# A fused attention, expert and feed-forward kernel: a feed-forward weight piece in five bit operations instead of six, with two pieces fetched ahead instead of four

## The chip, the cores and the metric

The kernel runs on one core of one Trainium2 chip. The metric is the device time of one execution in microseconds. The engines are named as in the profile: PE is TensorE (PEld its weight loads), DVE is VectorE, ACT is ScalarE, POOL is GpSimd and SP is SyncE, whose queue issues most transfers.

## The reference

```python
x = attention(q, k, v, f)                 # causal softmax with a decay, 4 x 8 heads, 576 x 64
x = x.transpose(0, 2, 1, 3).reshape(2304, 512)
logits = x @ w_gate + modality_bias[modality_id]
e_idx = argmax(logits, axis=1)            # one of 8 experts for each token
gate_w = softmax(logits)[e_idx]
for e in range(8):
    h = maximum(x[e_idx == e] @ w1[e], 0)             # 512 -> 1024
    out[e_idx == e] = gate_w * (h @ w2[e])            # 1024 -> 512
h = out @ w_in                                        # 512 -> 2048
g = maximum(h, 0) + alpha * minimum(h, 0)
return g @ w_out                                      # 2048 -> 512
```

The two feed-forward weights `w_in` and `w_out` arrive as 64-bit floats: they are drawn as 32-bit numbers and divided by a 64-bit square root. The kernel reads each number as two 32-bit words, `lo` and `hi`, and rebuilds a 32-bit float from them: the sign and the top exponent bit of `hi`, the next 27 bits of `hi` shifted left by 3, and the top 3 bits of `lo`.

## The kernel before, in words

Products are computed in pairs of 16-bit numbers, a high part and the rest (`split`), so that each matrix product is three matmul passes. Attention and routing fill the first part of the program. Tokens are then gathered by expert into slots of 128 rows. The changed code lies in the loop at L1529, which runs once for each of the last 14 slots, `s` from 6 to 19. All five engines run in the order in which the program is written (`manual_schedule`), so an instruction that waits holds up everything behind it on its engine or queue.

One pass of the loop does the following. POOL gathers the tokens of slot `s + 4`. PE computes the first expert product of slot `s + 1` in two halves (`hidden`, L1197), and ACT (L1204) and DVE (L1205) turn each half into the 16-bit pair `hs`. SP issues a transposing transfer for the tokens of slot `s + 3` (`xturn`, L1180) and two for the pair of slot `s + 1` (`hturn`, L1218, `ht<-hs`). PE then computes the second product of slot `s` (`outer`, L1232), which reads the `ht` of that slot; ACT (L1244) and DVE (L1245) write its result `yr`, and POOL scatters it (L1249). `hs` and `ht` have two buffers each. After slot 14 SP also fetches the first rows for the feed-forward stage (`fetch_rows` of `x2a`, L1424), which needs the scatters so far.

Between these steps the loop prepares weights. `work` (L1502) is a list of 34 pieces: 26 feed-forward pieces, and after every third of them one of 8 pieces of a third expert's weights. So pieces 1, 5, 9, 13, 17, 21, 25 and 29 are expert pieces. Each piece has three steps: a fetch on SP of 512 KB into one of four buffers (`ffn_fetch` L1441, `part_fetch` L190 and L193); a second step (`ffn_bits` on DVE, or `part_hi`, two copies on ACT, L1492 and L1493); and a third (`ffn_split`: two ACT copies, L1475 and L1476, and a POOL subtraction, L1477; or `part_lo`: one POOL subtraction, L1498). `convert` with counter `k_` runs the second step of piece `k_`, the third step of piece `k_ - 1`, and one fetch. The counter `due` places one or two calls of `convert` ahead of `outer` and one or two behind it, mostly three in a pass. The calls are placed, by piece: slot 6: 0, 1 and 2; slot 7: 3, 4 and 5; slot 8: 6 and 7, 8; slot 9: 9 and 10; slot 10: 11, 12 and 13; slot 11: 14 and 15, 16; slot 12: 17 and 18, 19; slot 13: 20 and 21; slot 14: 22, 23 and 24; slot 15: 25 and 26, 27; slot 16: 28 and 29; slot 17: 30, 31 and 32; slot 18: 33 (the word "and" stands for `outer`).

A buffer of the four comes free when its feed-forward piece has been through `ffn_bits`, or its expert piece through `part_lo`, one call of `convert` later.

The feed-forward stage behind the loop prepares six more pieces with the same `ffn_bits` and `ffn_split` (`late_step`, L1707), between its own products (`ffn_in`, L1669, L1674 to L1682).

Of the kernel before, what the change touches and what calls it, by code (L numbers as in the profile page):

```python
# [17 lines left out]
ALU = mybir.AluOpType  # L18
# [70 lines left out]
LEAST = struct.unpack("f", struct.pack("I", 897 << 20))[0]  # L89
# [3 lines left out]
def kernel(  # L93
# [17 lines left out]
    nc = tc.nc  # L111
    B, H, S, D = q.shape
    N, DM = out.shape
    E, _, F = w1.shape
# [1151 lines left out]
    def wsel(s):  # L1266
        if s < NX:
            c = s // NA
            return (lambda m, kk, cs_: w1c[:, c, m, kk, cs_]), (lambda m, kk: w2c[:, c, m, kk, :])
        if s == NS - 1:  # L1270
            return (lambda m, kk, cs_: w1x[:, m, kk, cs_]), (lambda m, kk: w2x[:, m, kk, :])
        if s not in cvs:
            cvs[s] = nc.tensor.value_load(cri[0:1, s - NX:s - NX + 1], min_val=0, max_val=1)
        cv = cvs[s]
        return (
            (lambda m, kk, cs_: w1c[:, bass.ds(cv, 1), m, kk, cs_]), (lambda m, kk: w2c[:, bass.ds(cv, 1), m, kk, :])
        )
# [168 lines left out]
    def ffn_bits(g, raw):  # L1446
        lo, hi = raw[:, :, 0], raw[:, :, 1]
        ta = cvs2[0].tile([P, 512], U32, tag="ta", name="ta")
        tb = cvs2[0].tile([P, 512], U32, tag="tb", name="tb")
        tk = ta.bitcast(F32)  # L1450

        nc.vector.tensor_scalar(out=ta, in0=hi, scalar1=0x7FFFFFFF, scalar2=None, op0=ALU.bitwise_and)  # L1452
        nc.vector.tensor_scalar(  # L1453
            out=tb, in0=hi, scalar1=0x80000000, scalar2=0x40000000, op0=ALU.bitwise_and, op1=ALU.bitwise_or
        )
        nc.vector.tensor_scalar(out=tk, in0=tk, scalar1=LEAST, scalar2=None, op0=ALU.max)  # L1456
        nc.vector.scalar_tensor_tensor(  # L1457
            out=tb, in0=lo, scalar=29, in1=tb, op0=ALU.logical_shift_right, op1=ALU.bitwise_or
        )
        nc.vector.tensor_scalar(  # L1460
            out=ta, in0=ta, scalar1=3, scalar2=0x7FFFFFFF, op0=ALU.logical_shift_left, op1=ALU.bitwise_and
        )
        nc.vector.tensor_tensor(out=ta, in0=ta, in1=tb, op=ALU.bitwise_xor)  # L1463
        return tk

    def ffn_split(g, tk):
# [36 lines left out]
    for g in range(KH + 16 - LATE):  # L1503
        work.append((lambda g=g: ffn_fetch(g), lambda t, g=g: ffn_bits(g, t), lambda t, g=g: ffn_split(g, t)))
        if g % PS == 0 and g // PS < KD + KF // 2:
            y = g // PS
            work.append((lambda y=y: part_fetch(ex2, y), lambda t, y=y: part_hi(y, t), lambda t, y=y: part_lo(y, t)))
# [3 lines left out]
    def fetch():  # L1511
        if at_[0] < len(work):
            got[at_[0]] = work[at_[0]][0]()
            at_[0] += 1

    def convert():
        k_ = at_[1]
        if k_ < len(work):
            got[k_] = work[k_][1](got[k_])
        if 0 <= k_ - 1 < len(work):  # L1520
            work[k_ - 1][2](got.pop(k_ - 1))
        fetch()
        at_[1] += 1

    for _ in range(4):
        fetch()
    per = len(work) / (NS - NX - 0.5)
    due = 0.0
    for s in range(NX - 1, NS):  # L1529
        if s + 4 < NS:  # L1530
            gather(s + 4, *colof(s + 4))
        if s + 1 < NS:
            m1, _ = wsel(s + 1)
            hidden(s + 1, 0, m1)
            hidden(s + 1, 1, m1)
            if s + 3 < NS:
                xturn(s + 3)
            hturn(s + 1)
        due += per / 2
        while at_[1] < min(due, len(work)):  # L1540
            convert()
        outer(s, wsel(s)[1])
        if s == NS - 6:

            fetch_rows(x2a, 0, G0)
            fetch_tokens(0, G0)
        due += per / 2
        while at_[1] < min(due, len(work)):
            convert()
    while at_[1] <= len(work):  # L1550
        convert()
# [6 lines left out]
    with tc.If(more > 0):  # L1558
# [3 lines left out]
        for e in range(E):  # L1562
# [7 lines left out]
            out=inb, in0=jr, in1=sx[:, :, 0:1].rearrange("p e o -> p o e").to_broadcast([P, 32, E]), op=ALU.is_ge  # L1570
        )
        nc.vector.tensor_tensor(
            out=inb2, in0=jr, in1=sx[:, :, 1:2].rearrange("p e o -> p o e").to_broadcast([P, 32, E]), op=ALU.is_ge
# [11 lines left out]
            out=ro, in0=ro, in1=sx[:, :, 0:1].rearrange("p e o -> p o e"), op=ALU.subtract  # L1585
# [19 lines left out]
        for c in (1, 2):  # L1605
            nc.vector.scalar_tensor_tensor(
                out=off[:, 0, :], in0=sel[:, c, :], scalar=noff[:, c - 1:c], in1=off[:, 0, :], op0=ALU.mult, op1=ALU.add
# [4 lines left out]
            out=inb2, in0=inb2, scalar=float(P), in1=off.to_broadcast([P, 32, E]), op0=ALU.mult, op1=ALU.add  # L1612
# [94 lines left out]
    def late_step():  # L1707
        if lbits:
            g, tk = lbits.pop(0)
            ffn_split(g, tk)  # L1710
        if lraw:
            g, raw = lraw.pop(0)
            lbits.append((g, ffn_bits(g, raw)))
        if late:
            g = late.pop(0)
            lraw.append((g, ffn_fetch(g)))
# [50 lines left out]
```

## Time and profile before

| | us |
|---|---|
| runs of the kernel | 931.6, 944.95, 931.2 (median 931.6) |
| the profiled execution | 936.06 |
| its span in the profile | 934.3 |

| engine | busy us | share of the span |
|---|---|---|
| PE | 805.8 | 86% |
| DVE | 530.4 | 57% |
| ACT | 347.6 | 37% |
| POOL | 343.3 | 37% |

The shares are means over stages with different limits: the loop with the changed code lies between about 376 and 541 us of the span. A row of the timeline gives start, duration, engine, line, operation, the tiles written and read, the count, and in brackets how long the engine had been idle and what released it. A row of waits gives the total, the number of times and the longest. The names of releasers are inferred; where a named engine had long been done, it was another.

### The profile page before, as it was taken

How to read it: one execution, taken by the hardware profiler on the slowest of the kernel's cores; microseconds unless marked ns; L12 is line 12 of the kernel's file. 1: busy time of each engine (PE TensorE's matmuls, PEld its weight loads, DVE VectorE, ACT ScalarE, POOL GpSimd, SP SyncE). 2: the span in 40 equal slices, each digit the busy share in tenths (PEclk: the TensorE clock that was granted, in tenths of full speed). 3: DMA queues.
4: the chain of work that ended last, by engine and by line, in shares of the span. 5: the costliest groups of instructions: out<-in, count | busy, mean ns of one | idle time of the engine just before them, and what ended most of it. 6: DMA issues, size and time to landing. Idle time of an engine off the chain costs nothing. (4 is left out here: it accounts for less than half of the span.)

```text
span 934.3 us, 15725 instructions
## 1 busy us (share of the span) xinstructions
PE 805.8 (86%) x5565; PEld 448.9 (48%) x5565; DVE 530.4 (57%) x1236; ACT 347.6 (37%) x670; POOL 343.3 (37%) x387
## 2 busy tenths in 40 slices
PE   4887958596997874989887999899999999999995
PEld 3776746474775432434332474344444444444442
DVE  6987869694875554588997869633035105402400
ACT  4885747564755323445453323211012102201200
POOL 4544344352435225545553444423124114302400
PEclk9998888897999987989998999999999999999998
DMA  7889999999761896999989344002002000000000
GB/s 149 171 148 187 161 127 209 179 151 159 126 113 41 153 130 166 274 220 222 248 221 233 92 123 114 12 12 46 24 22 46 12 23 12 1 23 22 1 23 22
DMA packets 226632, 103.17 MB, mean 110 GB/s; under 512 B 192843, under 2 KB 213944, under 8 KB 226554
## 3 DMA queue, kind: packets, MB, share of 16 engines
q1 hardware_dynamic: 221018, 87.29, 50.2%
q0 software_dynamic: 5536, 14.86, 5.2%
q8 instruction: 46, 0.75, 0.4%
q14 instruction: 32, 0.26, 0.1%
HBM read 49.06 MB, written 15.59 MB: 69 GB/s over the span
## 5 line engine op out<-in xcount | busy, mean ns | idle before, releaser
L1674 DVE TENSOR_SCALAR t<-a,al 128x512 f32<-128x512 f32 (+1 forms) x80 | 55.6, 696 | 208.4 <-PE a L1669 208.4
L1669 PE MATMUL a<-x,wi 128*128 128x512 f16 x768 | 166.7, 379 | 0.1
L1669 PEld LDWEIGHTS <-wi 128*128 128x128 f16 x960 | 94.7, 99 | 98.6 <-issue 5.3
L1232 PE MATMUL y<-wcc,ht 128*128 (+1 forms) x456 | 113.0, 405 | 33.3 <-DMA ht<-hs 33.2
L1691 PEld LDWEIGHTS <-g 128*128 128x128 f16 x864 | 84.9, 98 | 106.9 <-issue 6.1
L1682 POOL TENSOR_TENSOR g<-t,g 128x512 f16<-128x512 f32 (+1 forms) x80 | 85.4, 1068 | 116.0 <-ACT g L1681 113.0
L1691 PE MATMUL o<-wo,g 128*128 128x512 f16 x540 | 120.7, 382 | 0.0
L1197 PE MATMUL h<-wcc,xgt 128*128 (+1 forms) x456 | 105.9, 387 | 16.2 <-POOL wcc L1399 13.2
L1681 ACT ACTIVATE g<-t 128x512 f16<-128x512 f32 (+1 forms) x80 | 46.9, 587 | 156.4 <-DVE t L1677 151.7
L1232 PEld LDWEIGHTS <-ht 128*128 128x128 f16 x480 | 48.8, 103 | 98.8 <-DMA ht<-hs 39.6
L651 ACT ACTIVATE t<-e,nm 128x512 f32<-128x512 f32 (+2 forms) x144 | 81.3, 602 | 21.2 <-DVE e L628 13.8
L663 PE MATMUL pt<-identf,t 128*128 128x128 f32 x384 | 65.6, 296 | 24.5 <-ACT t L651 16.1
L1197 PEld LDWEIGHTS <-xgt 128*128 128x128 f16 x480 | 47.2, 99 | 73.3 <-issue 17.2
L679 DVE SCALAR_TENSOR_TENSOR p<-pt,p 128x512 f16<-128x512 f32 x96 | 65.4, 682 | 25.6 <-ACT p L672 25.0
L1691 PE MATMUL o<-wob,g 128*128 128x512 f16 x324 | 73.6, 380 | 3.4 <-ACT wob L1475 1.8
L1698 POOL DMA_INDIRECT out_dram<-ob,tka x18 | 17.6, 976 | 155.1 <-ACT ob L1696 155.1
L1696 ACT ACTIVATE ob<-o 128x512 f32<-128x512 f32 x18 | 10.7, 597 | 162.5 <-PE o L1691 162.5
L628 DVE TENSOR_SCALAR_CACHE_REDUCE e<-s 128x512 f32<-128x512 f32 (+3 forms) x128 | 58.0, 480 | 3.9 <-PE s L581 3.9
L672 ACT ACTIVATE p<-pt 128x512 f16<-128x512 f32 x96 | 56.1, 585 | 3.6 <-PE pt L663 3.3
L663 PEld LDWEIGHTS pt<-identf,t 128*128 128x128 f32 x384 | 43.3, 149 | 28.3 <-ACT t L651 19.6
L1677 DVE SCALAR_TENSOR_TENSOR t<-a,t 128x512 f32<-128x512 f32 (+1 forms) x80 | 51.0, 638 | 2.8
L580 PE MATMUL s<-yw,wcc 128*128 128x256 f16 (+1 forms) x192 | 48.1, 275 | 4.9 <-DMA yw<-wcc 4.9
(317 smaller groups left out, 1219.3 us busy)
## 6 DMA issues: line engine op xcount, KB each, us to landing
raw<-in_moe_w_in_dram SPq DMA_DIRECT2D x16, 512.0 KB, 6.7
raw<-in_moe_w_out_dram SPq DMA_DIRECT2D x16, 512.0 KB
yw<-wcc SPq DMA_DIRECT2D x14, 320.0 KB, 5.2
kn<-in_k_dram SPq DMA_DIRECT2D x16, 256.0 KB, 4.1
qn<-in_q_dram SPq DMA_DIRECT2D x32, 128.0 KB, 4.2
vn<-in_v_dram SPq DMA_DIRECT2D x16, 256.0 KB, 3.1
xs<-nat SPq DMA_DIRECT2D x16, 256.0 KB, 7.4
ht<-hs SPq DMA_TRANSPOSE x40, 3.2
```

Source lines behind the costliest of these rows:

```text
L628: nc.vector.tensor_scalar(out=e[:, c0:c0 + w], in0=ps[:, c0:c0 + w], scalar1=-1.0 / 8.0, scalar2=3.0e38, op0=ALU.mult, op1=ALU.min, accum_ ...
L651: nc.scalar.activation(out=natural(t[:, c0:c0 + w]), in_=halves(e[:, c0:c0 + w]), func=AF.Exp, scale=-1.0, bias=nm[:, y:y + 1])
L663: nc.tensor.transpose(pt[:, c * P:(c + 1) * P], e[:, c * P:(c + 1) * P], identf)
L672: nc.scalar.activation(out=p[:, 0, 0:512], in_=U[u][0], func=AF.Copy, scale=SP)
L679: nc.vector.scalar_tensor_tensor(out=p[:, 1, 0:512], in0=U[u][0], scalar=SP, in1=p[:, 0, 0:512], op0=ALU.mult, op1=ALU.subtract)
L1197: nc.tensor.matmul(hps, lhsT=xgt[:, kk, l, :], rhs=m1(m, kk, cs_), start=(kk == 0 and y == 0), stop=(kk == KD - 1 and y == 2),)
L1232: nc.tensor.matmul(yps, lhsT=ht[:, kk // (KF // 2), l, kk % (KF // 2), :], rhs=m2(m, kk), start=(kk == 0 and y == 0), stop=(kk == KF - 1 a ...
L1669: nc.tensor.matmul(hps[:, 0:n], lhsT=wi[:, mm, kk, m * P:(m + 1) * P], rhs=x2[:, l, kk, 0:n], start=(kk == 0 and y == 0), stop=(kk == KD - ...
L1674: nc.vector.tensor_scalar(out=t[:, 0:n], in0=hps[:, 0:n], scalar1=0.0, scalar2=al[:, m:m + 1], op0=ALU.min, op1=ALU.mult)
L1677: nc.vector.scalar_tensor_tensor(out=t[:, 0:n], in0=hps[:, 0:n], scalar=0.0, in1=t[:, 0:n], op0=ALU.max, op1=ALU.add)
L1682: nc.gpsimd.tensor_tensor(out=g[:, 1, 0:n], in0=t[:, 0:n], in1=g[:, 0, 0:n], op=ALU.subtract)
L1691: nc.tensor.matmul(ops, lhsT=g[:, l, t * P:(t + 1) * P], rhs=wo[m // (KH - LATE)][:, mm, m % (KH - LATE), :], start=(m == 0 and y == 0), s ...
```

## The change

`ffn_bits` builds the float in another order. Before, sign and top bit came from one DVE operation, `lo` was joined to them by a second, the shifted middle bits were made by a third, and an exclusive or joined the two. Now the masked and shifted middle bits come first, a `scalar_tensor_tensor` joins sign and top bit from `hi`, and a second one joins the bits of `lo`. `convert` issues its fetch ahead of its other two steps, and two fetches instead of four precede the loop, so the fetch in call `k` is that of piece `k + 2` and no longer `k + 4`. The number of buffers stays at four.

```diff
         nc.vector.tensor_scalar(out=ta, in0=hi, scalar1=0x7FFFFFFF, scalar2=None, op0=ALU.bitwise_and)
+        nc.vector.tensor_scalar(out=tk, in0=tk, scalar1=LEAST, scalar2=None, op0=ALU.max)
+
         nc.vector.tensor_scalar(
-            out=tb, in0=hi, scalar1=0x80000000, scalar2=0x40000000, op0=ALU.bitwise_and, op1=ALU.bitwise_or
-        )
-        nc.vector.tensor_scalar(out=tk, in0=tk, scalar1=LEAST, scalar2=None, op0=ALU.max)
+            out=tb, in0=ta, scalar1=3, scalar2=0x3FFFFFF8, op0=ALU.logical_shift_left, op1=ALU.bitwise_and
+        )
         nc.vector.scalar_tensor_tensor(
-            out=tb, in0=lo, scalar=29, in1=tb, op0=ALU.logical_shift_right, op1=ALU.bitwise_or
-        )
-        nc.vector.tensor_scalar(
-            out=ta, in0=ta, scalar1=3, scalar2=0x7FFFFFFF, op0=ALU.logical_shift_left, op1=ALU.bitwise_and
-        )
-        nc.vector.tensor_tensor(out=ta, in0=ta, in1=tb, op=ALU.bitwise_xor)
+            out=tb, in0=hi, scalar=0xC0000000, in1=tb, op0=ALU.bitwise_and, op1=ALU.bitwise_or
+        )
+        nc.vector.scalar_tensor_tensor(
+            out=ta, in0=lo, scalar=29, in1=tb, op0=ALU.logical_shift_right, op1=ALU.bitwise_or
+        )
         return tk
...
     def convert():
+
         k_ = at_[1]
+        fetch()
         if k_ < len(work):
             got[k_] = work[k_][1](got[k_])
         if 0 <= k_ - 1 < len(work):
             work[k_ - 1][2](got.pop(k_ - 1))
-        fetch()
         at_[1] += 1
 
-    for _ in range(4):
+    for _ in range(2):
         fetch()
```

## Rows read from the trace of the kernel before

**Rows 1.** Busy time by engine, granted clock and DMA share, of the loop and behind it.
```profile
core 0: us, PE busy (x) PEld busy (x) DVE busy (x) ACT busy (x) POOL busy (x), PEclk, DMA share, GB/s
376.00:541.60 165.60, 144.06 (x637) 63.22 (x636) 134.33 (x207) 72.18 (x110) 78.83 (x86) 0.96 0.85 211
541.60:601.00 59.40, 53.94 (x334) 33.56 (x335) 51.50 (x84) 18.50 (x36) 29.11 (x32) 0.97 0.35 91
```

**Rows 2.** Waits of PE in the loop, 376 to 541.4 us.
```profile
PE y L1232 <- DMA ht<-hs: 19.3, 9, 7.0
```

**Rows 3.** Timeline of PE in the loop.
```profile
403.94 8.21 PE L1232 MATMUL y<-wcc,ht 128*128 x24 [3.28 <-DMA ht<-hs]
...
451.68 5.34 PE L1232 MATMUL y<-wcc,ht 128*128 x24 [2.60 <-DMA ht<-hs]
...
504.00 7.68 PE L1232 MATMUL y<-wcc,ht 128*128 x24 [7.00 <-DMA ht<-hs]
...
533.97 5.35 PE L1232 MATMUL y<-w2x,ht 128*128 128x512 f16 x24 [1.57 <-DMA ht<-hs]
```

**Rows 4.** Waits of SP's queue in the loop, 376 to 541.6 us.
```profile
SPq L193 <- POOL w2x L1498: 7.5, 1, 7.5
...
SPq L1424 <- DMA ys<-yr,dpos: 6.3, 1, 6.3
...
SPq L1441 <- POOL wo L1477: 0.3, 1, 0.3
```

**Rows 5.** Timeline of SP's queue, 394 to 416 us.
```profile
394.92 7.67 SPq L1218 DMA_TRANSPOSE ht<-hs  x2
...
409.84 0.34 SPq L190 DMA_DIRECT2D wst__6252<-in_moe_w_dram  x1
...
411.61 3.28 SPq L1218 DMA_TRANSPOSE ht<-hs  x2
```

**Rows 6.** Waits of DVE, 395 to 500 us.
```profile
DVE yr L1245 <- ACT yr L1244: 5.8, 4, 1.7
DVE hs L1205 <- ACT hs L1204: 4.0, 3, 1.4
```

**Rows 7.** Timeline of DVE: one piece through its bit operations.
```profile
381.71 0.42 DVE L1456 TENSOR_SCALAR ta<-ta 128x512 f32<-128x512 f32 x1
382.04 0.68 DVE L1457 SCALAR_TENSOR_TENSOR tb<-raw,tb 128x512 uint32<-128x512 uint32 x1
382.64 0.42 DVE L1460 TENSOR_SCALAR ta<-ta 128x512 uint32<-128x512 uint32 x1
383.09 0.69 DVE L1463 TENSOR_TENSOR ta<-ta,tb 128x512 uint32<-128x512 uint32 x1
```

**Rows 8.** Timeline of DVE and POOL, 389 to 394 us.
```profile
390.55 2.85 DVE L1460 TENSOR_SCALAR ta<-ta 128x512 uint32<-128x512 uint32 x1
...
390.98 2.13 POOL L1498 TENSOR_TENSOR w1x<-wst__6017,w1x 128x1024 f16<-128x1024 f32 x1
```

**Rows 9.** Timeline of DVE behind the loop: one late piece begins, and the next product.
```profile
575.66 0.88 DVE L1452 TENSOR_SCALAR ta<-raw 128x512 uint32<-128x512 uint32 x1
...
580.72 0.74 DVE L1674 TENSOR_SCALAR t<-a,al 128x512 f32<-128x512 f32 x1
```

**Rows 10.** Fetches of feed-forward pieces (L1441): time from issue to landing.
```profile
DMA to landing us min/median/max: 5.0/6.7/8.4
```

**Rows 11.** Timeline of ACT: the use of piece 5.
```profile
400.89 1.04 ACT L1492 ACTIVATE w1x<-wst__6090 128x1024 f16<-128x1024 f32 x1
```

**Rows 12.** Timeline of SP's queue, 484 to 512 us.
```profile
485.75 1.02 SPq L1441 DMA_DIRECT2D raw<-in_moe_w_out_dram  x2
493.14 1.97 SPq L1424 DMA_TRANSPOSE x2a<-ys  x1
...
495.83 0.42 SPq L1441 DMA_DIRECT2D raw<-in_moe_w_out_dram  x1
```

**Rows 13.** Timeline of DVE, 494 to 517 us.
```profile
494.58 0.42 DVE L1452 TENSOR_SCALAR ta<-raw 128x512 uint32<-128x512 uint32 x1
...
512.49 0.75 DVE L1245 SCALAR_TENSOR_TENSOR yr<-y,gs,yr 128x512 f16<-128x512 f32 x1 [2.79 <-ACT yr L1244]
516.24 0.69 DVE L1205 SCALAR_TENSOR_TENSOR hs<-h,hs 128x512 f16<-128x512 f32 x1 [3.01 <-ACT hs L1204]
```

## The prediction

> **What bounds the kernel now.** I read the table of busy time by stretch first. The changed code works in the loop, 376 to 541.6 us, 165.6 us long; there PE is busy for 144.06 us, DVE for 134.33, and the DMA engines for 0.85 of the time, so three resources are near their limit at once [rows 1]. Then the waits of PE: 19.3 us in nine waits, all at the second product, which waits for the transposed `ht` [rows 2]. The timeline of PE puts places to them: 7.00 us at 504.0 and 1.57 us at the last slot have causes of their own (below), so 19.3 - 7.0 - 1.57 = 10.7 us are left in seven waits, and the 24 matmuls behind the one of 3.28 us took 8.21 us where others take 5.34, another 2.9 us [rows 3].
>
> Why is `ht` late? The waits of SP's queue answer half of it. Thirteen of their rows are fetches (L1441, L190, L193) that wait for a buffer; they run from 7.5 down to 0.3 us and sum to 46.9 us [rows 4]. The fetch in call `k` takes the buffer of piece `k`, which is only now being converted, and for an expert piece comes free one call later on POOL. The transposes stand behind it: a fetch was issued only at 409.84, and the two `ht` transfers followed at 411.61 [rows 5]. The other half is the DMA engines: the `ht` pair at 394.92 took 7.67 us to issue by itself, where the one at 411.61 took 3.28 [rows 5].
>
> The waits of DVE say what that is worth. From 395 to 500 us DVE waits only 5.8 + 4.0 = 9.8 us, for results of PE that ACT passes on [rows 6]. For the rest it goes from piece to `hs` to piece without a break, so in this stretch the loop can't become more than 9.8 us shorter unless DVE's own work does.
>
> **The bit operations.** One operation of 0.42 us goes from each of 32 pieces, 26 in the loop and 6 behind it. What counts is the distance from start to start. An operation that doesn't need its predecessor's result starts before that ends: 381.71 to 382.04 is 0.33 us for 0.42, and 382.04 to 382.64 is 0.60 for 0.68. One that needs it starts after the end: 382.64 to 383.09 is 0.45 us for the same 0.42 [rows 7]. In the old order only the last operation needs the one right ahead of it: 0.34 + 0.33 + 0.34 + 0.60 + 0.45, and 0.61 for the last, is 2.67 us. In the new order each operation needs the one ahead: 0.45 + 0.45 + 0.45 + 0.71 + 0.61 = 2.67 us. The saving is nothing. If the gaps vanished, 0.34 + 0.34 + 0.34 + 0.60 + 0.61 = 2.23 us would save 0.44 us x 26 = 11.4 us of DVE in the loop; if each dependent start cost another 0.1 us, 4 x 0.1 x 32 = 12.8 us would be lost. I take nothing, since rows 7 are the same engine, shapes and types.
>
> The Trainium skill, "VectorE: DVE Perf Modes", section "The DRAIN you can't avoid", states that the next DVE operation does not start until the pipe is empty, whatever the semaphores, and advises to minimize the count of operations. By that rule the order costs nothing and one removed operation saves its whole time. The hand-overs of rows 7 speak against it.
>
> DVE's stalls stay as well. While POOL subtracts, a DVE operation stands: 2.85 us beside a POOL operation of 2.13 us [rows 8]. POOL's work is unchanged, one subtraction for each feed-forward piece. In the new order two operations of 0.6 to 0.7 us stand last; a subtraction that meets them a little sooner or later moves a piece by up to 0.4 us either way, x 26 = 10 us at most; I take 0. Behind the loop DVE is busy for 51.50 of 59.4 us and the chain that ended last runs through it [rows 1]; a late piece holds it from 575.66 to 580.72, 5.06 us against the 2.67 worked out above, the first operation alone 0.88 instead of 0.42 [rows 9]. POOL's subtractions there are as many in either order, so I take 0 there too; the bounds are 6 x 0.34 = 2.0 us either way.
>
> **The fetches.** Fetch `k + 2` needs the buffer of piece `k - 2`, done two calls earlier. The 46.9 us of SP's waits nearly vanish. Two fetches fewer, 1 MB, also stand ahead of the first transposes, and in later passes the fetches go out right behind `ht` instead of just ahead of the next one. So most of the seven waits of PE should go: a gain of at most 10.7 + 2.9 = 13.6 us, at least nothing. DVE gives most of it back, because an earlier second product only lets it reach `yr` sooner (rows 6: 5.8 us of waits in that place); the waits for `hs` follow PE's own pace. I keep 4 us.
>
> The change adds waits for data. A fetch lands 5.0 to 8.4 us after issue, 6.7 in the middle [rows 10]. Where three calls fall in a pass with two ahead of `outer` (slots 6, 7, 10, 14 and 17), the third piece is now fetched in the pass that uses it: pieces 2, 5, 13, 24 and 32. Piece 5: its fetch would stand behind the `ht` pair of 394.92, be issued at about 398 and land at 404.7, where ACT used it at 400.89 [rows 5, 11]: 3.8 us late. Queued behind it on ACT are its second copy, the copies of piece 4 and both `hs` of the next slot, for which DVE and then the transposes wait. The same holds for 13; for 2, 24 and 32, which wait on DVE with `hs` behind them, I get 0 to 3 us. Part is absorbed, since earlier `ht` leave slack for a later `hs`, and a POOL subtraction that ran beside DVE's bits now falls into its wait. I charge 1 us each for two of them, 2 us; the bounds are 0 and 5 x 3.8 = 19 us.
>
> One more is moved past another wait on SP: piece 26. Its fetch was issued with the pair at 485.75; now it stands behind the fetch of `x2a`, which is released at 493.1 by a scatter, in the place of 495.83 [rows 12]. It lands at 502.5, where its bits began at 494.58: 8 us late, and piece 27, behind the next `ht` pair, about as late. Queued behind both on DVE is `hs` of slot 17. What covers it: DVE waits 2.79 and 3.01 us in the next pass anyway, and PE's 7.00 us at 504.0, which also come from the `x2a` wait, stay [rows 3, 13]. I take 0; without the cover it is 8 us.
>
> **Sum.** 0 for the bits, -4 and +2 for the fetches: -2 us on the profiled execution's 936.1 (934.3 of span and 1.8 around it), 934. That execution is 4.5 us over the median of the runs shown, 931.6; in terms of that median I predict 930 us, which is no change that can be told.
>
> **Rivals.** *SP's queue was the whole cost* (faster). PE gets all 13.6 us back, and DVE keeps up because an operation less does count, 0.34 x 26 = 8.8 us, which also brings the scatter ahead of `x2a` forward; with 2.0 us behind the loop that is up to 20 us: 912 to 922. For it: 46.9 us of waits that go. Against it: rows 6 and 7. This is the case in which the page's rule holds. Chance 0.18, of which 0.06 below 913.
>
> *Two pieces are too few* (slower). With the DMA engines at 0.85, fetches land at the slow end, 8.4 us, and the `ht` pair ahead of them takes as long to issue as at 394.92. Then five passes pay about 3 us each, 26 and 27 together 8 us more, 23 in all, less the 4 kept: 938 to 951. It decides once DVE's waits for `raw` exceed the 9.8 us that it waited before. For it: rows 5 and 10. Against it: but for 26 and 27 and those five, every piece is fetched a pass ahead. Chance 0.22, of which 0.07 above 950.
>
> *The change doesn't do what it says*: `ht` is late through the DMA engines alone and the fetch waits were harmless. Then nothing moves: 931.6, inside the forecast.
>
> **How the numbers follow.** The forecast, with the harmless case, has 0.60 and its own range 923 to 937: -8 is more of the 9.8 us kept, +6 a larger charge for late pieces. Two per cent, about what a measurement of this kernel can tell from no change, is 18.6 us: below 913 or above 950. Faster 0.06, within 0.87, slower 0.07. The range for 8 in 10 takes in most of both rivals: 914 to 946.
>
> **What would show it.** In the new profile the fetch lines' waits on SP fall from 46.9 to under 10 us. Each new bit operation starts 0.03 us after the one ahead of it, with about 11 us less busy DVE in the loop but a loop about as long. PE's waits for `ht` at 403.9 and 451.7 shrink; the 7 us behind `x2a` stay. DVE or ACT waits for `raw` or an expert piece at 2, 5, 13, 26 and 27, and at few others. I am wrong if the five operations overlap like independent ones, if DVE waits for data in most passes, or if the loop ends more than 8 us earlier or later.

## The result: 936.06 us, some half a per cent slower

| | changed kernel | kernel before, same chip | ratio [95% interval] |
|---|---|---|---|
| first comparison, 21 runs each | 936.06 | 930.21 | 1.0078 [1.0056, 1.0100] |
| on a second chip | 948.61 | 943.67 | 1.0038 [1.0012, 1.0063] |
| on a third chip | 935.09 | 931.50 | 1.0063 [1.0029, 1.0098] |

The ratios are taken from fast runs of both kernels in turns and are not the quotients of the two medians beside them, which are 1.0063, 1.0052 and 1.0039.

The change costs 0.4 to 0.8%, that is 4 to 7 us. It stays within the 2% that count as no change, and 936 lies inside the forecast's own range, but the forecast had a gain of 2 us and all three intervals lie above 1.

### The profile page after: what moved, and what is told of

The parts are those of the page before. It is cut to its first block, busy times and chain, and to the rows that moved or that the text cites. A ratio compares the mean times of both kernels' runs of the same rounds, so it can differ in the third digit from the quotient of the medians.

```text
span 936.1 us, 15675 instructions
## 1 busy us (share of the span) xinstructions
PE 804.4 (86%) x5561; PEld 447.7 (48%) x5565; DVE 529.6 (57%) x1204; ACT 347.6 (37%) x670; POOL 345.7 (37%) x387
## 5 line engine op out<-in xcount | busy, mean ns | idle before, releaser
L1675 DVE TENSOR_SCALAR t<-a,al 128x512 f32<-128x512 f32 (+1 forms) x80 | 55.6, 695 | 208.6 <-PE a L1670 208.6
L1670 PE MATMUL a<-x,wi 128*128 128x512 f16 x768 | 166.6, 379 | 0.0
L1670 PEld LDWEIGHTS <-wi 128*128 128x128 f16 x960 | 94.7, 99 | 98.1 <-issue 4.8
L1197 PE MATMUL h<-wcc,xgt 128*128 (+1 forms) x456 | 109.8, 395 | 24.0 <-POOL wcc L1399 16.2
L1232 PE MATMUL y<-wcc,ht 128*128 (+1 forms) x456 | 109.2, 395 | 24.3 <-DMA ht<-hs 24.2
L1682 ACT ACTIVATE g<-t 128x512 f16<-128x512 f32 (+1 forms) x80 | 46.9, 587 | 155.5 <-DVE t L1678 150.8
```

The costliest lines, as they stand in the source:

```text
L1197: nc.tensor.matmul(hps, lhsT=xgt[:, kk, l, :], rhs=m1(m, kk, cs_), start=(kk == 0 and y == 0), stop=(kk == KD - 1 and y == 2),)
L1232: nc.tensor.matmul(yps, lhsT=ht[:, kk // (KF // 2), l, kk % (KF // 2), :], rhs=m2(m, kk), start=(kk == 0 and y == 0), stop=(kk == KF - 1 a ...
L1670: nc.tensor.matmul(hps[:, 0:n], lhsT=wi[:, mm, kk, m * P:(m + 1) * P], rhs=x2[:, l, kk, 0:n], start=(kk == 0 and y == 0), stop=(kk == KD - ...
L1675: nc.vector.tensor_scalar(out=t[:, 0:n], in0=hps[:, 0:n], scalar1=0.0, scalar2=al[:, m:m + 1], op0=ALU.min, op1=ALU.mult)
```

## The profile after

In the changed kernel the bit operations keep lines 1452 to 1461, and the lines behind `convert` move by one (L1669 becomes L1670, L1674 becomes L1675). The same table of busy time by stretch, of the loop and of what follows [rows 1]:

```profile
core 0: us, PE busy (x) PEld busy (x) DVE busy (x) ACT busy (x) POOL busy (x), PEclk, DMA share, GB/s
376.20:544.40 168.20, 146.31 (x638) 63.64 (x636) 132.88 (x181) 71.95 (x110) 82.09 (x87) 0.95 0.83 208
544.40:603.80 59.40, 54.72 (x337) 33.88 (x338) 49.91 (x78) 18.52 (x37) 29.39 (x32) 0.96 0.35 91
```

The loop takes 168.2 us instead of 165.6, and behind it nothing is lost. The two profiled executions, 937.88 and 936.06 us, lie closer together than the medians, so they show only part of the 4 to 7 us. DVE has 26 instructions fewer and only 1.45 us less busy time. The timeline of DVE, one piece through the new order [rows 7]:

```profile
522.74 0.42 DVE L1452 TENSOR_SCALAR ta<-raw 128x512 uint32<-128x512 uint32 x1
523.20 0.43 DVE L1453 TENSOR_SCALAR ta<-ta 128x512 f32<-128x512 f32 x1
523.66 0.43 DVE L1455 TENSOR_SCALAR tb<-ta 128x512 uint32<-128x512 uint32 x1
524.12 0.69 DVE L1458 SCALAR_TENSOR_TENSOR tb<-raw,tb 128x512 uint32<-128x512 uint32 x1
524.85 1.53 DVE L1461 SCALAR_TENSOR_TENSOR ta<-raw,tb 128x512 uint32<-128x512 uint32 x1
```

From start to start it is 0.46, 0.46, 0.46 and 0.73 us: every operation begins 0.03 to 0.04 us after its predecessor's end. (The last one stands for 1.53 us beside a subtraction of POOL; undisturbed it takes 0.69.) Waits of SP's queue in the loop, fetches and `x2a` alone [rows 4]:

```profile
SPq L1424 <- DMA ys<-yr,dpos: 9.2, 1, 9.2
...
SPq L1441 <- DVE ta L1461: 3.2, 2, 1.7
SPq L193 <- POOL w2x L1498: 3.2, 2, 2.7
...
SPq L1441 <- DVE ta L1452: 0.7, 1, 0.7
```

The fetches' 46.9 us have become 3.2 + 3.2 + 0.7 = 7.1. The wait ahead of `x2a` has grown from 6.3 to 9.2 us, since the queue now reaches it sooner. The queue has not become free by this: its waits ahead of the `ht` transposes (L1218), all put down to DVE, grew from 47.3 to 72.7 us. Waits of PE over the loop, and where they fall in its timeline [rows 2, 3]:

```profile
PE y L1232 <- DMA ht<-hs: 14.2, 5, 5.3
PE h L1197 <- DVE hs L1205: 5.3, 3, 2.6
```

```profile
399.41 5.34 PE L1232 MATMUL y<-wcc,ht 128*128 x24
...
421.77 4.44 PE L1197 MATMUL h<-wcc,xgt 128*128 x12 [2.57 <-DVE hs L1205]
...
458.42 4.17 PE L1197 MATMUL h<-wcc,xgt 128*128 x12 [2.54 <-DVE hs L1205]
...
501.59 8.19 PE L1232 MATMUL y<-wcc,ht 128*128 x24 [5.28 <-DMA ht<-hs]
...
535.20 6.77 PE L1232 MATMUL y<-w2x,ht 128*128 128x512 f16 x24 [4.71 <-DMA ht<-hs]
```

The wait of 3.28 us at 403.94 is gone: that product now starts at 399.41, with no wait. What PE gained there it waits out elsewhere: 5.3 us for `hs` of DVE, a wait that the loop did not have, and 4.71 instead of 1.57 at the last slot. 14.2 + 5.3 is 19.5 us, against 19.3 before.

The timeline of SP's queue, and then that of DVE, at the pieces behind the `x2a` fetch [rows 12, 13]:

```profile
480.94 0.57 SPq L1441 DMA_DIRECT2D raw<-in_moe_w_out_dram  x1
482.18 0.39 SPq L193 DMA_DIRECT2D wst__6982<-in_moe_w_dram  x1
491.86 2.01 SPq L1424 DMA_TRANSPOSE x2a<-ys  x1
...
494.59 0.41 SPq L1441 DMA_DIRECT2D raw<-in_moe_w_out_dram  x1
```

```profile
499.61 3.15 DVE L1452 TENSOR_SCALAR ta<-raw 128x512 uint32<-128x512 uint32 x1 [4.41 <-DMA raw<-in_moe_w_out_dram]
...
505.83 0.43 DVE L1452 TENSOR_SCALAR ta<-raw 128x512 uint32<-128x512 uint32 x1 [0.69 <-DMA raw<-in_moe_w_out_dram]
...
509.41 1.28 DVE L1205 SCALAR_TENSOR_TENSOR hs<-h,hs 128x512 f16<-128x512 f32 x2
...
514.28 0.74 DVE L1245 SCALAR_TENSOR_TENSOR yr<-y,gs,yr 128x512 f16<-128x512 f32 x1
516.27 1.29 DVE L1205 SCALAR_TENSOR_TENSOR hs<-h,hs 128x512 f16<-128x512 f32 x2 [1.24 <-ACT hs L1204]
```

Piece 26 is asked for at 494.59, and DVE stands 4.41 us for it; piece 27 costs another 0.69. Three more waits for data are on record, piece 2 on DVE and expert pieces 5 and 13 in the timeline of ACT:

```profile
389.59 0.43 DVE L1452 TENSOR_SCALAR ta<-raw 128x512 uint32<-128x512 uint32 x1 [0.52 <-DMA raw<-in_moe_w_in_dram]
```

```profile
402.04 1.06 ACT L1492 ACTIVATE w1x<-wst__6182 128x1024 f16<-128x1024 f32 x1 [0.43 <-DMA wst__6182<-in_moe_w_dram]
438.43 1.06 ACT L1492 ACTIVATE w1x<-wst__6519 128x1024 f16<-128x1024 f32 x1 [1.69 <-DMA wst__6519<-in_moe_w_dram]
```

That makes 0.52 + 0.43 + 1.69 + 4.41 + 0.69 = 7.7 us of waits for weight data in the loop that the kernel before did not have, 5.6 of them on DVE. (ACT also waits 3.9 us for piece 1, where it waited 4.4 before.)

## Experiments

The theory: the operations are worth nothing because DVE pays at the hand-overs what it saves on the operation; the fetch order loses because data come late, and an engine that sets the pace has no slack to cover that. The rivals: the new order of operations is itself slower; the loss is `x2a` alone; SP's freed queue is what counts. Ratios are to the kernel before on the same chip. One kernel measured on two chips differs by up to 0.48%, where an interval reaches 0.2 to 0.35% to either side, so kernels are compared within a chip where that is possible. "Loop" is the time in the profiled execution from the first fetch's issue to the first feed-forward matmul; before: 165.6 us. It comes from one execution of each kernel; three executions of the changed kernel, on three chips, gave 168.2, 171.7 and 170.3.

| kernel | chip | ratio [95%] | loop us |
|---|---|---|---|
| five operations, old fetches | A | 0.9985 [0.9961, 1.0009] | 163.9 |
| six operations, new fetches | A | 1.0052 [1.0024, 1.0080] | 169.4 |
| changed, `x2a` behind a call of `convert` | A | 1.0037 [1.0016, 1.0057] | 168.4 |
| three ahead, five buffers | A | 0.9907 [0.9880, 0.9935] | 162.7 |
| the same, six operations | B | 0.9945 [0.9916, 0.9974] | 165.5 |
| changed, hand-overs loosened | B | 0.9880 [0.9846, 0.9915] | 159.7 |
| three ahead, five buffers, `x2a` late | B | 0.9972 [0.9943, 1.0001] | 162.5 |
| changed | B | 1.0038 [1.0012, 1.0063] | 171.7 |
| changed, `x2a` late | B | 0.9990 [0.9964, 1.0015] | 167.7 |
| three ahead, five buffers, pairs | B | 1.0041 [1.0012, 1.0069] | 170.8 |
| three ahead, five buffers | B | 0.9953 [0.9926, 0.9980] | 162.3 |
| three ahead, four buffers | B | 0.9965 [0.9931, 1.0000] | 162.5 |
| changed | C | 1.0063 [1.0029, 1.0098] | 170.3 |
| changed, `x2a` late | C | 1.0038 [1.0004, 1.0071] | 165.6 |
| three ahead, four buffers | C | 0.9999 [0.9970, 1.0028] | 162.3 |
| the same, hand-overs loosened | C | 0.9801 [0.9757, 0.9845] | 154.2 |

On chip B the four lines from "changed, `x2a` late" to "three ahead, four buffers" ran in another set than the four above them.

### Either half of the change alone

```diff
 # five operations, old fetches (against the changed kernel)
-        fetch()
         if k_ < len(work):
...
+        fetch()
         at_[1] += 1
-    for _ in range(2):
+    for _ in range(4):
```

> The kernel before with the five bit operations alone; fetches as before, four ahead. Theory A (late data is the loss, the bit operations are neutral): ratio to before 0.998 to 1.002, DVE starts one operation 0.45 us after the one before it, no wait of DVE for raw. Theory B (the bit operations are the loss, since now two operations with two SBUF inputs stand last and meet POOL's subtraction): ratio 1.005 to 1.010, and the mean from piece to piece grows by 0.1 us or more.

Measured: 0.9985, 1.4 us of gain whose interval holds zero; PE waits 18.3 us for `ht`, SP's fetch waits are there as before, and DVE waits 0.2 us for data.

```diff
 # six operations, new fetches: ffn_bits as before the change, convert() as after
```

> The kernel before with the fetch order alone, two pieces ahead and the fetch first in each call; six bit operations as before. Theory A (late data is the loss): ratio 1.005 to 1.010, DVE waits some 5 us for raw, most of it at piece 26 behind the fetch of x2a. Theory B (the bit operations are the loss): ratio 0.998 to 1.002.

Measured: 1.0052, a loss of 4.9 us, with DVE's waits over the loop:

```profile
DVE ta L1452 <- DMA raw<-in_moe_w_out_dram: 7.2, 2, 5.6
DVE ta L1452 <- POOL wi L1477: 1.4, 1, 1.4
DVE ta L1452 <- DMA raw<-in_moe_w_in_dram: 0.6, 1, 0.6
```

The halves add to 3.5 us of loss. It comes from the fetches; the new order of operations is not what is slower. ACT waits 2.1 and 0.6 us for pieces 13 and 5 here too.

### Where the late data come from

```diff
 # x2a behind a call of convert
         outer(s, wsel(s)[1])
+        due += per / 2
+        while at_[1] < min(due, len(work)):
+            convert()
         if s == NS - 6:
...
-        due += per / 2
-        while at_[1] < min(due, len(work)):
-            convert()
```

> The changed kernel with the fetch of x2a and its tokens moved behind the second group of calls in its pass, so that the fetch of piece 26 no longer stands behind the wait for the scatter. Theory A in its narrow form (pieces 26 and 27 are most of the loss): the wait of DVE for raw near 500 us falls from 4.4 us to under 1 us and the ratio to before falls from 1.008 to 1.000 to 1.004. Theory A in its wide form (many small delays) or theory B: the ratio stays at 1.006 to 1.010.

Measured: 1.0037, which is inside the range for the narrow theory; but the changed kernel itself did not run on chip A, so whether this is a gain is open, and the wait did not go away. Piece 26 was on time at 498.22, and piece 27 took its place. The timeline of DVE:

```profile
498.22 0.44 DVE L1452 TENSOR_SCALAR ta<-raw 128x512 uint32<-128x512 uint32 x1
...
507.61 0.43 DVE L1452 TENSOR_SCALAR ta<-raw 128x512 uint32<-128x512 uint32 x1 [6.58 <-DMA raw<-in_moe_w_out_dram]
```

One piece later, and 6.58 us instead of 4.41: with two ahead, the piece asked for behind the long wait of the queue is late, whichever of the two it is. So the fetch of `x2a` was moved away altogether:

```diff
 # x2a late
-        outer(s, wsel(s)[1])
-        if s == NS - 6:
+        if s == NS - 2:
             fetch_rows(x2a, 0, G0)
...
+        outer(s, wsel(s)[1])
```

> The changed kernel with the fetch of the late token rows moved from the sixth-last slot of the loop to the second-last one; two pieces ahead and four buffers stay. Theory A (the loss is pieces 26 and 27, asked for behind that fetch's wait): VectorE's waits for raw fall from 5.1 us to under 1.5 and the ratio to before is 0.997 to 1.002. Theory B (two pieces ahead are too few anyway, other pieces are late in turn): the waits for raw stay above 3 us and the ratio stays at 1.004 to 1.008.

Measured on chip B: 0.9990, waits for `raw` of 1.5 us for `w_in` and 0.7 for `w_out`, 2.2 in all. The ratio lies in the range of theory A, the waits between the bounds that I gave the two. To read it beside the others it ran again on chip C, with the changed kernel and three pieces ahead.

> The changed kernel beside the three others of this set: ratio 1.003 to 1.008, as the two times before.

> The changed kernel with the late rows' fetch moved to the second-last slot, beside it on one chip. Theory A (the two pieces behind that fetch are the whole loss of the fetch order): it lies 0.7 to 1.1% under the changed kernel and within 0.2% of three ahead. Theory B (they are about half of it, the rest is that a third piece ahead covers every other late read too): 0.3 to 0.6% under the changed kernel, three ahead 0.2 to 0.4% lower still.

Measured on chip C: 1.0063 for the changed kernel and 1.0038 with `x2a` late, 0.25% under it. On chip B it is 0.48% (1.0038 and 0.9990, in two sets). The intervals overlap in each case; the sign is the same twice. On chip C that is just under the range of theory B. The move has a price of its own, though: it brings `hs` of slot 18 forward by 6.3 us on chip C (135.0 us into the loop instead of 141.3) and by 5.1 on chip B, and loses some at the end, where the first feed-forward product, which reads `x2a`, waits 4.6 and 4.8 us instead of 2.4. So its ratio tells too little of what pieces 26 and 27 cost. Behind this move ACT waits 1.3 and 0.6 us for pieces 13 and 5, as in the changed kernel, since nothing has changed for them.

### One piece more ahead

```diff
 # three ahead, four buffers
-    for _ in range(2):
+    for _ in range(3):
         fetch()
```

> The changed kernel with three pieces ahead at the loop's start, but four buffers. The fetch then takes the buffer that the piece before has just given up, so SP waits for POOL's or VectorE's last operation on it. Theory A (the data are late only behind the late rows' fetch, and time ahead is what lacks): the waits for raw fall below 2 us and the ratio is 0.992 to 0.998. Theory B (the queue's waits come back with a full set of buffers, and hold up what stands behind them): SP's waits for buffers are above 20 us again, and the ratio is 0.998 to 1.004.

> The changed kernel with three pieces ahead in the four buffers, beside it on one chip. If what is lost is time ahead: 0.6 to 1.2% under the changed kernel, with VectorE's waits for raw under 2 us. If it is a matter of the chip: within 0.3% of it.

Measured: 0.9965 on chip B; on chip C 0.9999, 0.64% (6.0 us) under the changed kernel beside it, with intervals that do not meet, but no faster than the kernel before. Waits for weight data that the kernel before did not have fall from 8.3 us in the changed kernel there to 1.7. The larger waits of SP's fetches over the loop, on chip C:

```profile
SPq L1441 <- DVE ta L1452: 12.8, 5, 4.9
SPq L1441 <- DVE ta L1461: 8.7, 6, 3.0
SPq L190 <- POOL w1x L1498: 8.1, 2, 5.0
SPq L193 <- POOL w2x L1498: 3.2, 1, 3.2
SPq L190 <- POOL yr L1248: 1.2, 1, 1.2
```

With one more of 0.6, 34.6 us of the queue's waits are back, and the loop is 8.0 us shorter than in the changed kernel. The two timelines of DVE at piece 26 and at `hs` of slot 18, with three ahead and then of the changed kernel on that chip:

```profile
495.29 4.05 DVE L1452 TENSOR_SCALAR ta<-raw 128x512 uint32<-128x512 uint32 x1 [1.73 <-DMA raw<-in_moe_w_out_dram]
...
508.84 0.69 DVE L1205 SCALAR_TENSOR_TENSOR hs<-h,hs 128x512 f16<-128x512 f32 x1 [1.57 <-ACT hs L1204]
```

```profile
497.41 3.14 DVE L1452 TENSOR_SCALAR ta<-raw 128x512 uint32<-128x512 uint32 x1 [4.23 <-DMA raw<-in_moe_w_out_dram]
...
514.16 1.29 DVE L1205 SCALAR_TENSOR_TENSOR hs<-h,hs 128x512 f16<-128x512 f32 x2 [1.24 <-ACT hs L1204]
```

The loops begin at 374.7 and 372.9 us. At `hs` of slot 18 three ahead is 508.8 - 374.7 = 134.1 us into its loop, the changed kernel 514.2 - 372.9 = 141.3.

With a fifth buffer the queue's waits are gone as well (two small tiles of a branch that is not taken share space to make room):

```diff
 # three ahead, five buffers
-    wst[0] = mid.enter_context(tc.tile_pool(name="wst3", bufs=4))
+    wst[0] = mid.enter_context(tc.tile_pool(name="wst3", bufs=5))
...
-    for _ in range(2):
+    for _ in range(3):
```

> The changed kernel with a fifth fetch buffer and three pieces ahead instead of two; every fetch still finds its buffer free. Room for the buffer comes from two small tiles of a branch that these inputs do not take. Theory A: DVE no longer waits for raw and ACT no longer for an expert piece, SP still waits under 10 us for buffers, ratio 0.990 to 1.000. Theory B (bit operations): the ratio stays at 1.006 to 1.010.

> The kernel with five operations, three pieces ahead and five buffers once more, beside the others: 0.988 to 0.994 if its gain is its own and not that chip's; 0.997 or more if it was not.

Measured: 0.9907 and 0.9953, faster than the kernel before on two chips, and on chip B than the changed one too; the second lies between the two ranges named for it. The fetches' waits on SP over the loop are 6.7 and 5.7 us, DVE waits 1.7 and 1.8 us for data. Beside four buffers on chip B it is 0.12% lower, less than either is known to.

```diff
 # the same, six operations: ffn_bits as before the change
```

> Five buffers and three pieces ahead, as in the run with the fifth buffer, but with the six bit operations of before. Theory A (all of the change in time is in the fetches, the bit operations are neutral): ratio to before 0.988 to 0.995, as with five operations (0.991). Rival (the five operations are worth something once no piece is late, because DVE is then the limit): ratio 0.996 or more.

Measured: 0.9945, a gain of 5 us with the old operations. It is not seen in the loop: in the one trace DVE waits 3.7 us for data there, and the loop is 165.5 us long, as it was before the change; the stretch behind it is 3.4 us shorter.

```diff
 # three ahead, five buffers, x2a late: the edits of both
```

> The kernel with the fifth buffer and three pieces ahead, and the fetch of x2a and its tokens moved from the pass of slot 14 to that of slot 18, between the transposes and the second product. If the wait for the scatter on SP's queue is what holds the transposes of slot 16: PE's wait of 3 to 7 us near 505 falls under 1 us, SP waits elsewhere for x2a without harm, and the ratio falls from 0.991 to 0.980 to 0.987. Rival (DVE sets the pace there anyway): the ratio stays at 0.988 to 0.993.

Measured: 0.9972, outside both ranges and no better than without that move. The timeline of PE:

```profile
505.72 5.34 PE L1232 MATMUL y<-wcc,ht 128*128 x24 [0.37 <-DMA ht<-hs]
...
538.70 8.28 PE L1232 MATMUL y<-w2x,ht 128*128 128x512 f16 x24 [6.04 <-DMA ht<-hs]
```

The 7.00 us at slot 16 [rows 3] are down to 0.37, and the last slot waits 6.04 us instead: a gap of PE's closed is not a gap of the loop closed.

### DVE's hand-overs

```diff
 # hand-overs loosened: each operation reads what was written two operations before
-        nc.vector.tensor_scalar(out=tk, in0=tk, scalar1=LEAST, ..., op0=ALU.max)
+        nc.vector.tensor_scalar(out=tb.bitcast(F32), in0=hi.bitcast(F32), scalar1=LEAST, ..., op0=ALU.max)
...
-            out=tb, in0=ta, scalar1=3, scalar2=0x3FFFFFF8, ...
+            out=ta, in0=ta, scalar1=3, scalar2=0x3FFFFFF8, ...
...
-            out=ta, in0=lo, scalar=29, in1=tb, ...
+            out=ta, in0=lo, scalar=29, in1=ta, ...
```

> The changed kernel with its five bit operations rearranged so that none reads the result of the one right ahead of it (each reads what was written two before); the weights that come out are wrong. Theory A (a dependent start costs 0.11 us, four of them eat the saved operation): starts 0.34 us apart instead of 0.45, a piece without POOL beside it takes 2.2 to 2.3 us instead of 2.7, and the ratio to before falls from 1.008 to 0.998 to 1.005, since DVE is near its limit in the loop. Rival (an operation starts when the one before it has left, whoever reads it): starts stay at 0.45 us and the ratio at 1.006 to 1.010.

> The changed kernel once more, on the same chip as the others of this call: ratio 1.005 to 1.010 as before.

Measured: 0.9880, beside 1.0038 for the changed kernel: 1.6% for five operations of the same shapes, more than expected. The timeline of DVE:

```profile
391.05 0.41 DVE L1453 TENSOR_SCALAR tb<-raw 128x512 f32<-128x512 f32 x1
391.38 0.42 DVE L1455 TENSOR_SCALAR ta<-ta 128x512 uint32<-128x512 uint32 x1
391.72 0.68 DVE L1458 SCALAR_TENSOR_TENSOR tb<-raw,tb 128x512 uint32<-128x512 uint32 x1
392.32 0.68 DVE L1461 SCALAR_TENSOR_TENSOR ta<-raw,ta 128x512 uint32<-128x512 uint32 x1
```

Starts lie 0.33, 0.34 and 0.60 us apart, each before its predecessor's end, where the changed kernel has 0.46, 0.46 and 0.73. And once more with three ahead:

> Three pieces ahead in four buffers, and each bit operation reads what was written two operations before, so the weights are not what they should be: it prices the hand-overs with no data late. Theory A (VectorE's hand-overs set the pace beside the fetches): 0.7 to 1.5% under three ahead with the true operations. Theory B (with VectorE faster the data are late again, or the transposes set the pace): within 0.5% of three ahead, with VectorE's waits for raw or TensorE's waits for ht grown by what it gained.

Measured: 0.9801, 2.0% under three ahead with the true operations, again more than expected; the loop is 154.2 us instead of 162.3, in an execution that was the slowest of its six (918.23, median 911.7). DVE waits for data a little longer (3.2 us for piece 26 instead of 1.7), so part of that is given back. With nothing but DVE's hand-overs changed, the loop is 8 to 12 us shorter: DVE sets the pace of this loop.

```diff
 # pairs: where two feed-forward pieces fall together, their operations alternate, behind the third step of the piece before
-            got[k_] = work[k_][1](got[k_])
+            got[k_], got[k_ + 1] = ffn_bits(None, got[k_], got[k_ + 1])
```

> The kernel with three pieces ahead and five buffers, and where two feed-forward pieces fall due in one call their bit operations stand alternately, so that each reads what was written two operations before. Theory A (VectorE's hand-overs set the pace of the loop): each pair saves ten or so hand-overs of 0.11 us each, about 0.9 us, eight pairs 7 us, of which the loop gives back most: ratio 0.980 to 0.987, loop length 156 to 159 us. Theory B (something else is next, or the pair keeps the feed-forward multiplications waiting): 0.990 to 0.996, with TensorE's waits for y or h on VectorE longer in its place.

Measured: 1.0041, against 0.9953 for the same kernel without pairs: a miss. The timeline of DVE at one pair:

```profile
426.46 0.42 DVE L1454 TENSOR_SCALAR ta<-raw 128x512 uint32<-128x512 uint32 x1
429.64 0.43 DVE L1454 TENSOR_SCALAR ta<-raw 128x512 uint32<-128x512 uint32 x1 [2.76 <-POOL wi L1483]
429.99 0.76 DVE L1456 TENSOR_SCALAR ta<-ta 128x512 f32<-128x512 f32 x2
```

The hand-overs do shrink (two operations in 0.76 us), but the second `ta` has to wait until POOL has subtracted an older piece, because `ta` has two buffers. Over the loop DVE waits 7.6 us for POOL and 4.1 for data, more than the 7 us to be saved. A third buffer for `ta` was not tried.

## Why the prediction missed

**The bit operations: right.** Nothing was taken, and 1.4 us [a gain of 3.6 to a loss of 0.8] was measured. A piece takes 0.46 + 0.46 + 0.46 + 0.73 + 0.61 = 2.72 us where 2.67 was worked out. The lower bound, hand-overs that vanish, is what the loosened kernels come near: 11.4 us were given for the loop, 12.0 and 8.1 us of loop measured. Operations that don't read the one ahead start 0.08 us before its end, those that do 0.03 us behind it, and that distance is worth more here than an operation.

Of the Trainium skill, "VectorE: DVE Perf Modes", section "The DRAIN you can't avoid", the prediction told only half: the section adds that a next operation that is not held starts earlier. The starts 0.33 us apart for 0.42 us agree with that half. The advice to minimize the count of operations stands in the page's section "Rules for kernel authors"; it does not carry here: one fewer in each piece gave 1.4 us, within the noise, and the same five with loosened hand-overs 1.6 to 2.0%.

**DVE's busy time: wrong view.** I said that it would fall by about 11 us. It fell by 1.45, because the table of busy time counts overlapping operations once. The overlap of the old order was in that number already.

**Behind the loop: right.** A late piece holds DVE 577.83 to 582.76, 4.93 us instead of 5.06, and the stretch from the first feed-forward matmul to the end is 0.9 us shorter. In the other two traces of the changed kernel that stretch is 2.7 and 3.0 us shorter, but with six operations and three ahead it is 3.4 us shorter too, so the operations are not what does it.

**The fetches' gain of 4 us: not refuted, not shown.** SP's waits went to 7.1 us as said, PE's waits at 403.9 and 451.7 went, and PE's sum stayed, as it would where DVE sets the pace. With three ahead, where data are hardly late, the ratio to the kernel before is 0.9907 to 0.9965 on chips A and B (with six operations 0.9945) and 0.9999 on chip C: a gain of nothing to 9 us. How much of this is the freed queue is open: on chip B, four buffers with 30 us of these waits and five with 6 us differ by 0.12%.

**The late pieces: this step failed.** "I charge 1 us each for two of them, 2 us", and for 26 and 27 "I take 0; without the cover it is 8 us". The places were right: 2, 5, 13, 26 and 27, and no others. ("Every piece is fetched a pass ahead" was not so of 8, 16 and 19, which are asked for two calls earlier in their own pass; they were on time.) The charges were not right: 7.7 us of waits for data, and on chip C one piece more ahead takes 6.6 us of such waits away and wins 6.0 us of time. The fetch order alone gives 1.0052 with two ahead and 0.9945 with three and a fifth buffer, which across two chips is 1.07%, 10 us. With 6 to 10 in place of the 2, the sum is 2 to 6 us of loss, and 4 to 7 were measured; the match is in part luck, since the 4 us of gain are not shown and a term is missing from the sum, that of the last two slots below.

The cover failed in an instructive way. It was there: of DVE's waits of 2.79 and 3.01 us behind those pieces [rows 13] the changed kernel kept 0 and 1.24, and it reached `hs` of slot 18 at 516.27, where the kernel before did at 516.24. But the same slack is what a kernel whose data are on time turns into its gain: three ahead reaches that `hs` 134.1 us into its loop, the kernel before 516.24 - 376.05 = 140.2. (With six operations and three ahead it is 140.0, with 3.7 us of waits for data, so this room is seen with the five operations alone.) I spent the slack twice, as the cover of a loss and as the room for the 4 us.

About 26 and 27 by themselves less is certain: moving `x2a` away is worth 0.25 and 0.48%, 2 to 4 us of time, each within its measurement, and 5 to 6 us up to `hs` of slot 18; where the data are on time the same move brings that `hs` forward by 2.1 us (131.9 instead of 134.0 us, five buffers, chip B). That leaves some 3 to 4 us for the two pieces, an estimate from one execution each. The rest is in pieces 2, 5 and 13, and in what a third piece ahead gives elsewhere. These were not parted.

**The last two slots: a term put at 0.** Up to `hs` of slot 18 the changed kernel had lost nothing in its first trace, so the 2.6 us by which its loop is longer lie behind that, where no weight data are late. From that `hs` to the end of the loop it is 25.4 us in the kernel before, and 28.1, 29.6 and 29.0 in the three traces of the changed one. The timelines of DVE, before and after, at the first operation behind `hs` of slot 18 and at `hs` of slot 19:

```profile
518.13 1.20 DVE L1452 TENSOR_SCALAR ta<-raw 128x512 uint32<-128x512 uint32 x1
...
530.04 1.28 DVE L1205 SCALAR_TENSOR_TENSOR hs<-h,hs 128x512 f16<-128x512 f32 x2
```

```profile
517.48 2.97 DVE L1452 TENSOR_SCALAR ta<-raw 128x512 uint32<-128x512 uint32 x1
...
531.24 1.28 DVE L1205 SCALAR_TENSOR_TENSOR hs<-h,hs 128x512 f16<-128x512 f32 x2
```

POOL's two subtractions there began at 515.82 before and ran in part while DVE waited for `hs`; now they begin at 516.90 and end at 520.16, beside that operation. From `hs` to `hs` it is 14.97 us instead of 13.80, and the last second product takes 6.77 us instead of 5.35 [rows 3]. The prediction named the first of these, "a subtraction that meets them a little sooner or later", and took 0. Late pieces are not the cause, since three ahead still takes 28.2 us for the stretch. The five operations with the old fetches take 25.5, six operations take 28.3 with two ahead and 25.5 with three, so it is neither half alone; the cause was not tested.

**The rivals.** "Two pieces are too few" names the mechanism that won, but not at its price: DVE waited 5.6 us for data, not the 9.8 from which I let it decide, and of the five passes with two calls ahead of `outer` three paid 0.4 to 1.7 us and two nothing, not 3 each. No such threshold shows: with waits below it, one piece more ahead still won 6 us on chip C. "SP's queue was the whole cost" is out: the change took 40 us of its waits away and lost time, and three ahead has 35 us of them and is faster than the changed kernel. (Its terms, 13.6, 8.8 and 2.0 us, make 24 us, where the text has up to 20.) The harmless case, in which the fetch waits cost nothing, is not excluded by itself: 30 against 6 us of them differ by 0.12%, and three ahead is level with the kernel before on chip C. It does not explain the loss.

## What to carry to other kernels

Where one engine sets the pace, price a late piece of data on it in full (here 6.6 us of waits less went with 6.0 us of time less), and count its slack once: what covers a loss can't be a gain too. When operations are taken out of a chain, sum the distances from start to start, not the durations; dropping one that overlapped and tying the rest together saved nothing here that could be told. A shorter prefetch frees a queue, but a queue's waits for buffers cost nothing here that could be told and a transfer asked for behind a wait of 9 us came 4.4 us late: look for the longest wait on the queue, and fetch far enough ahead to pass it.

## What was not expected of the hardware

One kernel's ratio to another, both measured in turns on one chip, can lie outside its interval on another chip: three ahead with five buffers gave 0.9907 and 0.9953, the `x2a`-late kernel 0.9990 and 1.0038. The order of the three that ran on both chips B and C was the same: the changed one, `x2a` late, three ahead. Part of this is the way the ratio is taken: by the quotient of the medians the same pairs are 0.9932 and 0.9947, and 0.9999 and 1.0018, and the sets differed as well as the chips. A difference of half a per cent therefore asks for both kernels in one set on one chip.
